# A retention layer and a two-matrix MLP in one kernel: attention steps of four blocks in place of three

## The chip, the cores and the metric

The kernel runs on one core of a Trainium2 chip. The core has five engines with instruction streams of their own: TensorE (PE, matmuls into the 8 banks of PSUM, with the weight loads, PEld, booked apart), VectorE (DVE), ScalarE (ACT), GpSimd (POOL) and SyncE (SP). POOL issues the loads that turn float32 into bfloat16 on the way, SP issues the output stores and the transposing DMAs. The metric is the device time of one execution in microseconds, lower is better.

## The reference

There are 8 batch entries, 8 heads, 576 tokens an entry and 64 channels a head. Each entry goes through retention, a causal attention without softmax that decays with the distance, and its 512 channels a token then go through an MLP with 2048 hidden channels.

```python
q, k, v: (8, 8, 576, 64);  x @ w_in: (4608, 512) @ (512, 2048);  w_out: (2048, 512)
gamma = 1.0 - 2.0 ** (-5.0 - np.arange(H))
Dmat = np.where(rel >= 0, gamma[:, None, None] ** rel[None, :, :], 0.0)
ret = scores * Dmat                       # scores = q @ k.T / 8
x = (ret @ v).transpose(0, 2, 1, 3).reshape(B * S, H * D)
h = x @ w_in
out = (h * (1.0 / (1.0 + np.exp(-1.702 * h)))) @ w_out
```

The decay factors into a part of the key's position and one of the query's: values are scaled by gamma to the power of minus their position (`scale_v`), outputs by gamma to the power of theirs (`gq`). So a block of 64 queries needs the scores inside its own block, masked to the lower triangle, and a running state, the sum of k times v over all earlier blocks of its entry.

## The kernel before

**The MLP.** The 4608 tokens are cut into 9 MLP chunks of 512. For each, 16 units of `hidden` (4 matmuls of 128x512, ACT applies the activation and writes `gT`) and 16 units of `project` (4 matmuls each; 4 units make 128 output rows, which ACT copies to `osb` and SP stores). Three buffers `osb` rotate. Each unit takes a PSUM bank; the banks named U, H0 and H1 rotate in `next_bank`. The second MLP chunk is done in two halves of 256 tokens (`hidden_half`, `units_half`), and between them two of its four output rows.

**The attention.** Entry 0 is done at the start in chunks of 128 rows. Entries 1 to 7 are done in steps that are put between MLP units, in an order written out by hand. An entry has 9 blocks of 64 tokens; a step is 3 blocks, so there are 21 steps (`NWIDE`). Its matmuls are 64x64x64 and use one of four quarters of PE each: row half by where the operands lie, column half by where the result goes. To use all four within one block, `load_shifted` (L222) puts the k and v of heads 4 to 7 64 rows lower than those of heads 0 to 3, as two DMAs a tensor and chunk; an entry takes 5 chunks of 128 rows.

**A burst** (L587) is what PE does for a step: values and inter (the product of queries and state `zw`) for the step that is finished (`m_out`), scores and states for the next one (`m_in`). A merged burst has both, and in some places at the start they stand apart: `(burst, None, m, ...)` does only the second half, `(step, m, False)` only the first. [...] Scores go to bank pair S, outputs to O and Z, states to W and to corners of the others. After it DVE multiplies the output into `xT` (`evac_wide`, L682), masks the scores (`mask_wide`), sums the states into `zacc` (`state_wide`) and casts them to `zw`.

**Order and queues.** `run` (L956) issues units and, after unit i, what `between[i]` lists. A unit that stands ahead of a `step` also waits for everything that the step needs (`needs`), so that a burst doesn't stop in its middle. Scores need q and k with channels on the partitions: `turn` does this for the first chunks on PE, `turn_dma` (L528) for the others by transposing DMAs on SP. After step m, `turn_step(m + 3)` puts the transposes of step m + 3 into SP's queue, where each waits for its load and holds up what stands behind it; and new loads go into POOL's queue. A load waits until the sixth load ahead of it has landed (`pace`, L206). Three entries of staging (`NST`) and 10 turned chunks (`NQK`) rotate.

```python
AHEAD = 6
def pace():
    return issued[-AHEAD] if len(issued) > 3 * NC + AHEAD else None
```

Of the kernel before, what the change touches and what calls it, by code (L numbers as in the profile page):

```python
# [11 lines left out]
B = 8  # L12
# [10 lines left out]
NWIDE = 3 * (B - 1)  # L23
NSTEP = B * NC
# [107 lines left out]
def bass_retnet_parallel__then__act_gelu_quick_kernel(  # L132
# [11 lines left out]
    with es:  # L144
# [10 lines left out]
        posj = sb("posj", [P, NC], FP32)  # L155
# [6 lines left out]
        vraw = sb("vraw", [P, H, NC], FP32)  # L162
        vfac = [sb(f"vfac{i}", [P, H, NC], FP32) for i in range(2)]
        zacc = sb("zacc", [P, 3, 2 * 128], FP32)
        zw = sb("zw", [P, NBLK, 2, 2, DH], BF16)
# [8 lines left out]
        smw = [t[:, 0 : 2 * 6 * 64].rearrange("p (a x n) -> p a x n", a=2, x=6) for t in sm_all]  # L174
# [7 lines left out]
        psA = ps("psA", [P, 5, 512])  # L182
# [5 lines left out]
        psB = ps("psB", [P, 3, 512])  # L188
        psH = [psB[:, i, :] for i in range(2)]
        psU = psB[:, 2, :]  # L190
        pairs = [(psS, ["S"]),
                 (psB[:, 0:2, :].rearrange("p a (h n) -> p a h n", h=HP), [("H", 0), ("H", 1)])]

        def wide(m):
            return 1 + m // 3, m % 3
# [13 lines left out]
        def load(b, c, what="qkv"):  # L209
            sl, rows = b % NST, ROWS[c]  # L210
            for nm, src, dst in (("q", q, st_q), ("k", k, st_k), ("v", v, st_v)):
                if nm not in what:
                    continue
                if b > 0 and nm != "q":
                    load_shifted(b, c, nm, src, dst)
                    continue
                s = src[b, :, 128 * c : 128 * c + rows, :].rearrange("h p d -> p h d")
                d = dst[0:rows, sl, c, :].rearrange("p (h d) -> p h d", d=DH)
                paced(R.op("POOL", lambda e, d=d, s=s: e.dma_start(d, s),  # L219
                           w=[(nm, sl, c)], dma=(nm, sl, c), own=pace()))  # L220

        def load_shifted(b, c, nm, src, dst):  # L222


            sl = b % NST
            parts = []
            for u, (lo, hi) in enumerate(((0, ROWS[c]), (64 if c == 0 else 0, 128))):
                d = dst[lo:hi, sl, c, 256 * u : 256 * u + 256].rearrange("p (h d) -> p h d", d=DH)
                t0 = 128 * c - 64 * u
                s = src[b, 4 * u : 4 * u + 4, t0 + lo : t0 + hi, :].rearrange("h p d -> p h d")  # L230
                parts.append((d, s))
            paced(R.op("POOL", lambda e: [e.dma_start(d, s) for d, s in parts],  # L232
                       w=[(nm, sl, c)], dma=(nm, sl, c), parts=2, own=pace()))

        def load_entry(b, first=0):
            for c in range(first, NC):
                load(b, c)
# [14 lines left out]
        def iota(t, name, pattern, base, mul):  # L252
            R.op("POOL", lambda e: e.iota(t.ap(), pattern, base=base, channel_multiplier=mul,
                                          allow_small_or_imprecise_dtypes=True), w=[name])
# [22 lines left out]
        def constants_first():  # L277
            iota(posj, "posj", [[128, NC]], 0, 1)
            iota(posa, "posa", [[1, 128]], 0, 0)
            R.op("DVE", lambda e: e.tensor_tensor(  # L280
                vraw.ap(), posj.ap().unsqueeze(1).to_broadcast([P, H, NC]),
                lnh.ap().unsqueeze(2).to_broadcast([P, H, NC]), ALU.mult),
# [13 lines left out]
            for hp in range(HP):  # L296
# [6 lines left out]
                vfac[0].ap(), vraw.ap(), float(QK_SCALE), ALU.mult), r=["vraw"], w=[("vfac", 0)])  # L303
# [9 lines left out]
        def constants_shifted():  # L313
            for r in range(2):
# [4 lines left out]
            R.op("DVE", lambda e: e.tensor_copy(vfac[1][:, 0:4, :], vfac[0][:, 0:4, :]),  # L319
                 r=[("vfac", 0)], w=[("vfac", 1)])  # L320
            for h in range(4, H):
                R.op("DVE", lambda e, h=h: e.tensor_single_scalar(
                    vfac[1][:, h, :], vfac[0][:, h, :], float(gamma(h) ** 64), ALU.mult),
                    r=[("vfac", 0)], w=[("vfac", 1)])
            for t, nm in ((st_k, "k"), (st_v, "v")):
                R.op("DVE", lambda e, t=t: e.memset(t[0:64, 1:NST, 0, 256:512], 0.0),
                     w=[(nm, sl, 0) for sl in range(1, NST)])

        def constants_third(a, b):
            for t, nm in ((st_q, "q"), (st_k, "k"), (st_v, "v")):  # L330
                R.op("DVE", lambda e, t=t: e.memset(t[64:128, a:b, 4, :], 0.0),
                     w=[(nm, sl, 4) for sl in range(a, b)])
# [37 lines left out]
        def constants_mask3():  # L370
            m = mask.ap().unsqueeze(1).unsqueeze(1).to_broadcast([P, 2, 2, 128])
            f = vfac[0].ap().rearrange("p (u t j) c -> p j t u c", u=2, t=2)
            for j in range(2):
# [3 lines left out]
                     r=["mask", ("vfac", 0)], w=mask3_keys)  # L377

        def scale_v(n, eng="DVE", to=None):
            b, c = divmod(n, NC)  # L380
            sl = b % NST
            t = st_v[:, sl, c, :].rearrange("p (h d) -> p h d", d=DH)
            f = vfac[min(b, 1)][:, :, c : c + 1].to_broadcast([P, H, DH])
            if n == 0:
                i = early(1).rearrange("p (h d) -> p h d", d=DH)
                R.op(eng, lambda e: e.tensor_tensor(t, i, f, ALU.mult),
                     r=[("vfac", 0)] + early_keys(1), w=[("v", sl, c)])
                return
            if to is None:
                R.op(eng, lambda e: e.tensor_tensor(t, t, f, ALU.mult),  # L390
                     r=[("vfac", min(b, 1))], w=[("v", sl, c)])
# [3 lines left out]
                 r=[("vfac", min(b, 1)), ("v", sl, c)], w=[v3_key])  # L395

        def sides(n):
            b, c = divmod(n, NC)
            return [(0, st_q, "q", b % NST, c), (1, st_k, "k", b % NST, c)]
# [123 lines left out]
        def turn(n, own=False):  # L523
            at = next_bank() if own else None
            transposes(n, at)
            evac_t(n, at)
# [559 lines left out]
```

## Time and profile before

| | us |
|---|---|
| median of 3 runs | 299.05 (298.82 to 299.48) |
| the profiled execution, its own time | 298.93 |
| its span, first to last instruction | 297.1 |
| PE busy | 291.1 (98%) |
| DVE busy | 123.1 (41%) |
| ACT busy | 125.9 (42%) |
| POOL busy, issuing DMAs for the most part | 151.6 (51%) |
| of PE: `project` 128x512 (544 matmuls) | 122.0 |
| of PE: `hidden` 128x512 (492 matmuls) | 108.9 |
| chain of waits, share of PE | 94% |

The page gives busy time by engine, the span in 40 slices of 7.4 us (each digit the busy share in tenths), and the chain of waits, which is followed back from the last instruction to whatever released each one. In the chain and in timelines a line has the start in us, the duration, the engine, the tile and the line of the kernel (L627 states, L599 values, L615 inter, L641 scores, L732 and L749 hidden, L765 project, L533 transposing DMAs). "DMA to landing" is the time from the issue of a DMA until its last piece has arrived.

### The profile page before, as it was taken

The numbers are of one execution on the slowest core, as the hardware profiler recorded it, in microseconds if no ns is written. First come the engines' busy times: TensorE is split into PE (matmuls) and PEld (weight loads), VectorE is DVE, ScalarE is ACT, GpSimd is POOL, SyncE is SP. The second block draws the span as 40 slices with busy tenths as digits, with TensorE's granted clock in tenths as the row PEclk, the third lists the DMA queues.
The fourth block names the chain that finished last, engine by engine and source line by source line (L and its number), as shares of the span: only waits on it lengthen the run. The fifth ranks groups of instructions, "written<-read, shape, count | busy, mean of one in ns | idle before, by whom it ended". The sixth has DMA issues, their size and how long they took to land.

```text
span 297.1 us, 7697 instructions
## 1 busy us (share of the span) xinstructions
PE 291.1 (98%) x3399; PEld 148.5 (50%) x3399; DVE 123.1 (41%) x221; ACT 125.9 (42%) x208; POOL 151.6 (51%) x205
## 2 busy tenths in 40 slices
PE   7799999999999999999999999999999999999996
PEld 3464455848544444544454445545454445444444
DVE  7769475454445435532615324245326504000012
ACT  6658426617256313540355045503660275026600
POOL 8975979989959887568984797000000000000000
PEclk9999999999999999999999999999999999999999
DMA  9999999999999999999999999904820200030012
GB/s 133 156 186 190 173 171 165 188 131 140 182 140 143 183 143 175 194 130 134 154 218 124 114 188 162 85 2 108 170 38 2 107 37 2 0 108 35 0 50 93
DMA packets 154850, 36.04 MB, mean 121 GB/s; under 512 B 145472, under 2 KB 150336, under 8 KB 154816
## 3 DMA queue, kind: packets, MB, share of 16 engines
q0 software_dynamic: 116304, 18.10, 94.1%
q1 hardware_dynamic: 38512, 17.44, 32.6%
q8 instruction: 27, 0.44, 0.6%
q14 instruction: 7, 0.06, 0.1%
HBM read 36.70 MB, written 9.44 MB: 155 GB/s over the span
## 4 chain that ended last, share of the span: by engine, by line
PE 94%; POOL 2%; DMA 2%; issue 0%; DVE 0%; POOLq 0%
PE psB L765 40%; PE psB L732 36%; PE psB L749 5%; PE psA L627 2%; DMA st_k<-in_k_dram 2%; PE psA L599 2%; PE psA L641 2%; PE psA L615 1%; PE psA L765 1%; PE psA L791 1%; PE psB L843 1%; PE psA L411 1%; POOL st_k L219 1%; POOL st_q L219 1%; POOL st_v L219 1%
## 5 line engine op out<-in xcount | busy, mean ns | idle before, releaser
L765 PE MATMUL psB<-w_out_sb,gT 128*128 128x512 bf16 x544 | 122.0, 380 | 0.0
L732 PE MATMUL psB<-xT,w_in_sb 128*128 128x512 bf16 x492 | 108.9, 379 | 0.0
L737 ACT ACTIVATE gT<-psB 128x512 bf16<-128x512 f32 x123 | 73.5, 597 | 38.4 <-PE psB L732 38.1
L765 PEld LDWEIGHTS psB<-w_out_sb,gT 128*128 128x128 bf16 x544 | 51.8, 98 | 60.2 <-DVE sm L696 0.3
L732 PEld LDWEIGHTS psB<-xT,w_in_sb 128*128 128x128 bf16 x492 | 47.5, 98 | 56.5
L685 DVE TENSOR_TENSOR xT<-psA,gq 128x768 bf16<-128x768 f32 x21 | 20.1, 958 | 115.3 <-PE psA L615 115.3
L232 POOL DMA_DIRECT2D st_k<-in_k_dram x70 | 52.5, 774 | 15.2 <-DMA st_k<-in_k_dram 10.9
L774 ACT ACTIVATE osb<-psB 128x512 f32<-128x512 f32 x31 | 18.5, 597 | 90.2 <-PE psB L765 86.8
L232 POOL DMA_DIRECT2D st_v<-in_v_dram x70 | 51.9, 767 | 5.7 <-DMA st_v<-in_v_dram 3.3
L219 POOL DMA_DIRECT2D st_q<-in_q_dram x39 | 34.8, 891 | 10.2 <-DMA st_q<-in_q_dram 7.6
L390 DVE TENSOR_TENSOR st_v<-st_v,vfac 128x512 bf16<-128x512 bf16 x36 | 23.3, 681 | 1.2 <-DMA st_v<-in_v_dram 1.2
L714 DVE TENSOR_TENSOR zacc<-zacc,psA 128x256 f32<-128x256 f32 x49 | 20.5, 419 | 6.9 <-PE psA L627 5.7
L696 DVE TENSOR_TENSOR sm<-psA,maskw 128x768 bf16<-128x768 f32 x21 | 19.9, 948 | 0.0
L749 PE MATMUL psB<-xT,w_in_sb 128*128 128x256 bf16 x128 | 15.0, 273 | 0.0
L777 DVE COPY osb<-psB 128x512 f32<-128x512 f32 x3 | 2.1, 692 | 29.7 <-PE psB L765 29.7
L749 PEld LDWEIGHTS psB<-xT,w_in_sb 128*128 128x128 bf16 x128 | 12.2, 98 | 1.7
L418 ACT ACTIVATE qk<-psA 128x1024 bf16<-128x1024 bf16 x8 | 8.2, 1022 | 9.8 <-PE psA L411 9.8
L599 PE MATMUL psA<-sm,st_v 64*64 64x64 bf16 x504 | 11.8, 195 | 0.3
L627 PE MATMUL psA<-st_v,st_k 64*64 64x64 bf16 x448 | 11.8, 199 | 0.0
L627 PEld LDWEIGHTS psA<-st_v,st_k 64*64 64x64 bf16 x448 | 7.5, 105 | 8.3 <-issue 7.8
L755 ACT ACTIVATE gT<-psB 128x512 bf16<-128x512 f32 x16 | 9.4, 599 | 5.0 <-PE psB L749 5.0
L615 PE MATMUL psA<-qk,zw 64*64 64x64 bf16 x448 | 11.1, 194 | 0.0
(103 smaller groups left out, 164.3 us busy)
## 6 DMA issues: line engine op xcount, KB each, us to landing
out_dram<-osb SPq DMA_DIRECT2D x35, 256.0 KB, 3.9
st_q<-in_q_dram POOLq DMA_DIRECT2D x31, 128.0 KB, 7.5
st_k<-in_k_dram POOLq DMA_DIRECT2D x57, 64.0 KB, 7.3
st_v<-in_v_dram POOLq DMA_DIRECT2D x57, 64.0 KB, 7.0
w_out_sb<-in_moe_w_out_dram POOLq DMA_DIRECT2D x4, 512.0 KB, 10.9
w_in_sb<-in_moe_w_in_dram POOLq DMA_DIRECT2D x3, 512.0 KB, 8.6
st_k<-in_k_dram POOLq DMA_DIRECT2D x4, 128.0 KB, 4.8
w_in_sb<-in_moe_w_in_dram POOLq DMA_DIRECT2D x2, 256.0 KB, 6.8
```

The source lines that it names most:

```text
L219: paced(R.op("POOL", lambda e, d=d, s=s: e.dma_start(d, s), w=[(nm, sl, c)], dma=(nm, sl, c), own=pace()))
L232: paced(R.op("POOL", lambda e: [e.dma_start(d, s) for d, s in parts], w=[(nm, sl, c)], dma=(nm, sl, c), parts=2, own=pace()))
L390: R.op(eng, lambda e: e.tensor_tensor(t, t, f, ALU.mult), r=[("vfac", min(b, 1))], w=[("v", sl, c)])
L627: i = e.matmul(psA[half(j), bank, off + 64 * t : off + 64 * t + 64], rows_of(st_k, m_in, g, u, h), rows_of(st_v, m_in, g, u, h), start=(t ...
L685: R.op("DVE", lambda e: e.tensor_tensor(xT[:, :, t0 : t0 + 192].rearrange("p (u j) n -> p u j n", u=2), psA[:, 2:4, 0:384].rearrange("p u ...
L696: R.op("DVE", lambda e: e.tensor_tensor(o, i, k, ALU.mult), r=["maskw"], w=[("sm", si(m))], ps=["S"])
L714: R.op("DVE", lambda e, to=to, src=src, was=was: e.tensor_tensor(to, was, src, ALU.add), r=[("zacc", (blk - 1) % 3)], w=[("zacc", blk)], p ...
L732: i = e.matmul(bank, w_in_sb[:, a, 128 * f : 128 * f + 128], xT[:, a, 512 * c : 512 * c + 512], start=(a == 0), stop=(a == 3))
L737: R.op("ACT", lambda e: e.activation(gT[c % 2][:, f, :], bank, AF.Gelu_apprx_sigmoid), w=[("gT", c % 2, f)], ps=[key])
L749: m = e.matmul(bank[:, 256 * i : 256 * i + 256], w_in_sb[:, a, 128 * (f + i) : 128 * (f + i) + 128], xT[:, a, a0 : a0 + 256], start=(a == ...
L765: i = e.matmul(bank, gT[c % 2][:, f, 128 * r : 128 * r + 128], w_out_sb[:, f, :], start=(f == 0), stop=(f == NF - 1))
L774: R.op("ACT", lambda e: e.activation(osb[m].ap(), bank, AF.Copy), w=[("osb", m)], ps=[key])
```

## The change

Entries 1 to 7 become one line of 63 blocks, loaded in 32 chunks of 128 rows without the shift; chunks 4, 13 and 22 hold the end of one entry and the start of the next. A step is four blocks, so there are 16 steps. In place of the two head groups of one block, an even and an odd block now fill the four quarters together: outputs of even blocks go to bank O, of odd blocks to Z; states of even blocks to W, of odd blocks to U (Z where the burst stands alone). U is lent by the MLP, whose units leave it alone around a merged burst (`without`), while banks are taken by the order of last use (`lru`). `project` units of one row now come one after the other on two banks. From the third MLP chunk on there are two steps a chunk, after units 10 and 24; in the second, steps are placed by hand again. Step 3 is marked urgent: its output goes ahead of the states on DVE. The mask covers 8 x 64 columns for each half instead of 6 x 64, and the second set of factors (`vfac[1]`), the zero fills of the shifted corners and the PE transpose of chunk 9 go.

```diff
-NWIDE = 3 * (B - 1)
-NSTEP = B * NC
+NLIN = (B - 1) * NBLK
+NWIDE = (NLIN + 3) // 4
+NLOAD = (NLIN + 1) // 2
...
+        smw = [t.ap().rearrange("p (a x n) -> p a x n", a=2, x=8) for t in sm_all]
...
-        psA = ps("psA", [P, 5, 512])
+        psA = ps("psA", [P, 6, 512])
...
-        psB = ps("psB", [P, 3, 512])
...
+        psU = psA[:, 5, :]
...
+        def slot(N):
+            return divmod((N + NC) % (NST * NC), NC)
+
+        def rows_in(N):
+            return min(128, 64 * (NLIN - 2 * N))
+
+        def load_next(N):
+
+            if N >= NLOAD:
+                return
+            sl, c = slot(N)
+            b, p0 = 1 + 128 * N // S, 128 * N % S
+            pieces = [(0, b, p0, min(128, S - p0))]
+            if pieces[0][3] < rows_in(N):
+                pieces.append((64, b + 1, 0, 64))
+            for nm, src, dst in (("q", q, st_q), ("k", k, st_k), ("v", v, st_v)):
+                parts = []
+                for lo, e0, t0, n in pieces:
+                    s = src[e0, :, t0 : t0 + n, :].rearrange("h p d -> p h d")
+                    parts.append((dst[lo : lo + n, sl, c, :].rearrange("p (h d) -> p h d", d=DH), s))
+                paced(R.op("POOL", lambda e, parts=parts: [e.dma_start(d, s) for d, s in parts],
+                           w=[(nm, sl, c)], dma=(nm, sl, c), parts=len(parts), own=pace()))
...
+        def turn_dma(N):
+            n = NC + N
+            rows = rows_in(N)
+            for a, t, nm, sl, c in sides(n)[::-1]:
+                R.op("SP", lambda e, a=a, t=t, sl=sl, c=c: e.dma_start_transpose(
                     out=qk[n % NQK][:, a, :, 0:rows], in_=t[0:rows, sl, c, :]),
                     r=[(nm, sl, c)], w=[("qk", n % NQK, a)], dma=("turn", n % NQK, a))
 
...
         def blocks(m):
-            return range(3 * (m % 3), 3 * (m % 3) + 3)
...
+            return [(G % 4, G, G % NBLK) for G in range(4 * m, min(4 * m + 4, NLIN))]
...
+            return sorted({G // 2 for _, G, _ in blocks(m)})
+
...
+        def zbanks(fresh):
+            return ((4, "W"), (3, "Z") if fresh else (5, "U"))
 
...
+                r += stored(m_in, "kv") + turned_keys(m_in, 0) + turned_keys(m_in, 1)
...
+            def pairs_of(m):
+                bs = blocks(m)
+                return [bs[i : i + 2] for i in range(0, len(bs), 2)]
+
+            def state(e):
+                first = opening()
+                for two in pairs_of(m_in):
+                    for u in range(2):
                         for t in range(2):
+                            for blk, G, g in two:
+                                if g == NBLK - 1:
+                                    continue
+                                at = 256 * (blk // 2) + 128 * u + 64 * t
+                                bank = zb[blk % 2][0]
+                                for j in range(2):
+                                    h = 4 * u + 2 * t + j
+                                    i = e.matmul(psA[half(j), bank, at : at + 64],
+                                                 rows_of(st_k, G, h), rows_of(st_v, G, h),
+                                                 start=first(bank, j), stop=False,
+                                                 skip_group_check=True)
                 return i
 
...
+            def inter(e, same):
+                i = None
+                for two in pairs_of(m_out):
+                    for u in range(2):
+                        for blk, G, g in two:
+                            if g == 0:
+                                continue
+                            j = G % 2 if same else 1 - G % 2
+                            for t in range(2):
+                                i = e.matmul(out_at(G, u, j, t), zw[half(j), (G - 1) % 8, u, t, :],
+                                             turned_of(G, j, 0, u, t),
+                                             start=False, stop=not same, skip_group_check=True)
+                return i
...
+                R.op("PE", state, r=stored(m_in, "kv"), ps=[key for _, key in zb])
...
                 done = R.op("PE", phase_x, r=ro, ps=["O", "Z"])
...
+                R.op("PE", score, r=turned_keys(m_in, 0) + turned_keys(m_in, 1), ps=["S"])
...
+                R.op("PE", lambda e: inter(e, False), r=ro, ps=["O", "Z"], own=done)
+                if urgent or m_in is None:
+                    evac_wide(m_out)
+            if m_in is not None:
+                state_wide(m_in, zb, cast == "ACT")
+                if m_out is not None and not urgent:
+                    evac_wide(m_out)
                 mask_wide(m_in)
+                if cast != "ACT":
+                    cast_wide(m_in)
...
+        def state_wide(m, zb, on_act):
+            for blk, G, g in blocks(m):
+                if g == NBLK - 1:
+                    continue
+                bank, key = zb[blk % 2]
+                src = psA[:, bank, 256 * (blk // 2) : 256 * (blk // 2) + 256]
+                to, was = zacc[:, blk, :], zacc[:, (blk - 1) % 4, :]
...
+        load_next(0)
         load_w_out(2)
-        load(1, 1)
+        load_next(1)
         load_w_out(3)
-        load_entry(1, 2)
-        load_entry(2)
+        for N in range(2, 10):
+            load_next(N)
...
 
-        turns = [1]
-
-        def next_bank():
-            turns[0] += 1
-            return wide_banks[(1, 2, 0)[turns[0] % 3]]
+        lru = [0, 1, 2]
+
+        def next_bank(without=()):
+            x = next(x for x in lru if x not in without)
+            lru.remove(x)
+            lru.append(x)
+            return wide_banks[x]
 
...
-            if m > 1:
+            for N in range(10, 15):
+                load_next(N)
+
+        def step(m, into=True, cast="DVE", urgent=False):
+            burst(m, m + 1 if into and m + 1 < NWIDE else None, cast, urgent)
+            if m > 0:
                 turn_step(m + 3)
-            for c in ((0,), (1, 2), (3, 4))[i]:
-                if b + NST < B:
-                    load(b + NST, c)
+            load_next(2 * m + 15)
+            load_next(2 * m + 16)
 
         def turn_step(m):
             if m < NWIDE:
-                b, i = 1 + m // 3, m % 3
-                for n, which in (((0, "k"), (0, "q"), (1, "k"), (1, "q")),
-                                 ((2, "k"), (2, "q"), (3, "k")),
-                                 ((3, "q"), (4, "k"), (4, "q")))[i]:
-                    turn_dma(NC * b + n, which)
+                for N in chunks(m):
+                    turn_dma(N)
 
...
         def run(units, between):
+            joined = [i for i in between for fn, *args in between[i]
+                      if fn is step and (len(args) < 2 or args[1])]
             for i, unit in enumerate(units):
                 ahead = []
                 for fn, *args in between.get(i, ()):
                     if fn is step:
                         ahead += needs(args[0], args[0] + 1 if (len(args) < 2 or args[1])
                                        and args[0] + 1 < NWIDE else None)
-                unit(ahead)
+                unit(ahead, (0,) if any(k <= i <= k + 3 for k in joined) else ())
                 while later:
                     later.pop(0)()
                 for fn, *args in between.get(i, ()):
                     fn(*args)
 
...
-        def units_o(c, rows, eng="ACT"):
+        def units_o(c, rows):
             banks = {}
 
             def unit(r, g):
-                def go(ahead):
+                def go(ahead, without):
                     if g == 0:
-                        banks[r] = next_bank()
-                    project(c, r, g, *banks[r], eng=eng, ahead=ahead)
+                        banks[r] = next_bank((0,))
+                    project(c, r, g, *banks[r], eng="ACT", ahead=ahead)
                 return go
-            first = rows[:3]
-            return ([unit(r, g) for g in range(4) for r in first]
-                    + [unit(r, g) for r in rows[3:] for g in range(4)])
+            return [unit(r, g) for r in rows for g in range(4)]
 
         first = {r: next_bank() for r in (1, 2, 3)}
         first[0] = wide_banks[3]
-        run([lambda ahead, r=r, g=g: project(0, r, g, *first[r], eng="ACT", ahead=ahead)
+        run([lambda ahead, without, r=r, g=g: project(0, r, g, *first[r], eng="ACT", ahead=ahead)
              for g in range(4) for r in range(4)],
             {1: [(tail_turn,)], 3: [(intra, 4)], 5: [(turn, 5), (tail_out,), (regroup, 2)],
              7: [(scale_v, 5), (turn, 6)], 8: [(scale_v, 6), (regroup, 3)], 9: [(burst, None, 0, "ACT")],
              12: [(turn, 7)], 13: [(step, 0, False)], 14: [(scale_v, 7)], 15: [(turn, 8)]})
+        turn_step(2)
         turn_step(3)
-        turn_step(4)
         run(units_half(1, 0),
-            {0: [(turn, 9, True), (scale_v, 8), (scale_v, 9)], 1: [(burst, None, 1, "ACT")],
-             5: [(step, 1)]})
-        run(units_o(1, (0, 1)), {3: [(scale, 3)], 5: [(step, 2, False)]})
-        run(units_half(1, 1), {2: [(burst, None, 3, "ACT")], 4: [(scale, 4)]})
-        run(units_o(1, (2, 3)), {0: [(step, 3, True, "ACT")], 5: [(step, 4, False)], 6: [(scale, 5)]})
...
+            {0: [(scale_v, 8)], 1: [(burst, None, 1, "ACT")], 5: [(step, 1, False)]})
+        run(units_o(1, (0, 1)), {3: [(scale, 2)], 6: [(burst, None, 2, "ACT")]})
+        run(units_half(1, 1), {1: [(scale, 3)], 5: [(step, 2)]})
+        run(units_o(1, (2, 3)), {2: [(scale, 4)], 5: [(step, 3, True, "DVE", True)]})
+
+        for c in range(2, NCH):
             at = {}
-            for i, m in enumerate(steps):
-                u = (5, 15, 25)[i] if len(steps) == 3 else (8, 22)[i]
-                at[u - 4] = [(scale, m + 1)]
-                at[u] = [(step, m)]
-            region(c, at)
-        run(units_h(NCH - 1), {})
-        for r in range(3):
-            bank = next_bank()
-            for g in range(4):
-                project(NCH - 1, r, g, *bank)
+            for u, m in ((10, 2 * c), (24, 2 * c + 1)):
+                if c < NCH - 1:
+                    at[u - 5] = [(scale, m + 1)]
+                    at[u] = [(step, m)]
+            rows = range(4) if c < NCH - 1 else range(3)
+            run(units_h(c) + units_o(c, rows), at)
         project_pieces(NCH - 1, 3, [(psA[:, 2, :], "O"), (psW, "W")])
```

## The prediction

> **What bounds the kernel now.** I read the page first: busy shares, then the 40 slices. PE is busy in all but the first and last slices and has its full granted clock; so has the DMA row up to about 200 us, and POOL up to about 165 us.
>
> ```profile
> PE   7799999999999999999999999999999999999996
> ...
> POOL 8975979989959887568984797000000000000000
> PEclk9999999999999999999999999999999999999999
> DMA  9999999999999999999999999904820200030012
> ```
>
> To see: PE sets the end, but for the first two thirds the DMA engines are as full as PE, so an earlier demand for data can't simply be met earlier. The chain of waits names nearly only PE; here is its stretch around one merged burst (88 small matmuls), between two MLP pieces:
>
> ```profile
> 75.42 0.86 PE psB L765 x4
> 76.29 0.19 PE psA L627 x8
> 76.47 0.13 PE psA L599 x16
> ...
> 77.11 0.07 PE psA L615 x6
> 77.18 4.42 PE psB L765 x20
> ```
>
> To see: 0.89 us from 76.29 to 77.18, no wait on either side. Asked for PE's waits from 55 to 90 us, the profile has none: every transposed chunk is in time today. How closely, SP's transposes and their times to landing tell (issue, duration on SP; then the issues of the stretches 69.1 to 69.3 us and 78.0 to 78.2 us):
>
> ```profile
> 67.95 1.19 SPq L533 DMA_TRANSPOSE qk<-st_k  x1
> 69.19 1.64 SPq L533 DMA_TRANSPOSE qk<-st_q  x1
> ...
> 78.11 1.31 SPq L533 DMA_TRANSPOSE qk<-st_q  x1
> ```
>
> ```profile
> qk<-st_q SPq DMA_TRANSPOSE x1, 6.7
> ```
>
> ```profile
> qk<-st_q SPq DMA_TRANSPOSE x1, 7.1
> ```
>
> To see: a transpose lands some 7 us after its issue (the page's median over all is 7.6). Chunk 3 of entry 2 is turned (k 6.6 us after 67.95, so at 74.6; q at 75.8) when PE opens the unit that needs its k at 75.42. That is 0.8 us of slack.
>
> **The change part by part.** The profiled execution is 297.1 us of span in 298.93 us (1.83 around it), 0.12 under the median of 299.05. Sums below go against 298.93.
>
> *Small matmuls.* Their number stays (504 values, 504 scores, 448 states, 448 inters). In the chain a merged burst of 88 takes 0.89 us and one of 96 (92.60 to 93.56) 0.96, so 8.2 ns a matmul; a gap of 0.09 us ahead of each is booked on the MLP piece. A burst of 128 is 0.89 + 40 x 0.0082 + 0.09 = 1.31 us. Blocks left out of a pair (no state after an entry's last block, no inter before its first) leave two of four tiles idle and save nothing. Before: 17 merged, 4 in only (0.51 to 0.58), 4 out only (0.71 to 0.78), 21.0 in the chain + 25 x 0.09 = 23.3 us. After: 13 merged (one 0.13 shorter), 3 in only at 0.66 + 0.09 (0.58 + 16 x 0.0082, less two waits of PE on itself), 3 out only at 0.90 + 0.09: 22.1. Gain 1.2, and 1.55 of gain lies after the third MLP chunk's start at 84.21 (before 16.9, after 11 x 1.31 + 1.0 - 0.1). The transpose of chunk 9 on PE goes: 8 matmuls, 0.45.
>
> *VectorE.* Four sums of 0.42 instead of three, two output multiplications of 0.69 (nearest row: L518, 512 elements) for one of 0.96, a mask of 1.22 (L441, 1024 elements) for 0.95, a cast of 0.9: some 6 us a step against PE's 13 to 15. Hidden, except at two places. (a) Step 1's mask: states end 0.5 us after the burst starts, 1.75 + 1.22 more makes 3.5; PE is there after 0.75 + 3 x 0.87 = 3.3: wait 0.25. (b) Step 3 is urgent: both outputs come ahead of the sums. From the burst's end 0.14 + 1.3 + 1.33 (block 17 is an entry's last: two sums and a copy) = 2.75. The fourth sum frees bank U, and the third MLP chunk's first unit takes just that bank (the order of use leaves it oldest), two units or 1.73 us after the burst: wait 1.0. Bounds: 0, if the first unit had another bank, and 1.5.
>
> *ScalarE.* With two MLP banks a unit's Gelu must end within the next unit: it starts 0.42 after the last matmul, takes 0.597, and PE comes back 1.08 after: fits, by some 0.02 us, and only one unit a chunk is so placed. Output copies of 0.597 per 3.46 us are covered. If the cover fails, 0.05 each, 0.4 in all. The last chunk's copies on ScalarE instead of VectorE are off the path.
>
> *Loads.* POOL issues one DMA for a tensor of a chunk instead of two halves: 70 + 70 + 39 instructions shrink by 70, at 0.77 each. Whether that brings data sooner depends on who is the limit. POOL never paused from 46 to 58 us; but the DMA engines had the work queued: time to landing rose from 3 us (issues of 44 to 47 us) to 7 (62 to 66) and 10 (76 to 80).
>
> ```profile
> 46.00:58.00 12.00, 11.92 (x263) 8.96 (x261) 5.05 (x9) 9.12 (x15) 12.00 (x17) 1.00 1.83 186
> 58.00:70.00 12.00, 11.92 (x133) 7.32 (x120) 5.35 (x8) 3.45 (x6) 10.76 (x16) 1.00 2.31 131
> ```
>
> (Busy time of PE, PEld, DVE, ACT, POOL; clock; DMA share, over 1 where transfers overlap; GB/s.) From the landing of the last load of chunk 3 (47.8) to the turned q at 75.8 I count 16.5 loads of 128 rows, 8 transposes and 4 output stores: 28.5 pieces in 28.0 us, 0.98 each. [...] POOL's wait of 3.3 us for a memset (L326) near 22 us goes too; next in line there is the DMA queue, which holds weights till 42 us, so nothing is counted.
>
> On SP the transposes of chunks 8 and 9 now stand ahead of the second MLP chunk's first two output stores, which go out at about 76 instead of 74.5; ScalarE wants their buffers back at 88 at the earliest and they land some 7 us after issue, so this is covered by 4 us.
>
> *Demand.* This decides. Steps of four blocks on the same places of the second MLP chunk want 12 blocks at 66.5, 16 at 72.5, 20 at about 81; before it was 12 at 70.4, 15 at 75.4, 18 at 86.7. A unit ahead of a step waits for all its keys, both chunks' q and k turned. Chunks numbered along the line from 0, the last load of chunk 3 lands at 48.3 (64 more rows). Turned q of chunk 5 has 18 pieces ahead (6 loads, 4 in flight past them by the pace of six, 4 transposes, 4 stores): 66. Of chunk 7: 28 pieces, 75.7; of chunk 9: 38, 85.5. The other bound is by latency: k of chunk 7 lands after 17 pieces at 65.0, q is issued 1.3 later, lands after 7.4: 73.7; chunk 9 (27 pieces): 83.5. I take the middle, 74.7 and 84.5, since both rows are equally near.
>
> The walk: the second MLP chunk starts at 51.1 (before 50.85, plus 0.08 and 0.20 on step 0's two bursts). First half 8 x 0.87 + 0.75 + 1.0 + 0.25 = 8.95: 60.1. Seven projection units: 66.1, burst 0.75 and a wait of 0.2 on chunk 5's turn, one unit: 67.9. Five half units: 72.3; wait for chunk 7 till 74.7, **2.4**. Unit, burst 1.31, two units, five units: 82.9; wait for chunk 9 till 84.5, **1.6**. Unit, burst, two units 3.9, bank U 1.0: 89.4, where before had 84.2. That is 5.2 later, less 1.55 gained afterwards: +3.65. Time 298.93 + 3.65 = 302.6; with the bounds of the turns 301.6 to 303.6. From there on loads are ahead (chunk 11 turned at about 96, wanted at 98).
>
> **The rivals.**
>
> *Data in time* (other side: faster). If the transposes of chunk 7 land by 72.3 and of chunk 9 by 80.1, only (a) and (b) stay: 84.2 + 1.0 at the third chunk, +1.0 - 1.55, so about 298.3. It decides from a piece time of 0.85 us down. For it: POOL's 12.00 of 12.00, and fewer, larger DMAs; against it: the DMA row at 9 and the rising time to landing. Chance 0.17.
>
> *One wait instead of two*: transposes overtake queued loads (issues at 76 to 80 us: loads 10, transposes 7.1 to 8.3), chunk 7 by 73.5, chunk 9 by 82: 299.5 to 300.9. Chance 0.14.
>
> *The clock drops in the wait.* With PE idle for 2.4 us or more the clock could be withdrawn and take some us to return. No run here shows it: the longest waits of before, up to 1.6 us near the start, left the granted clock at 1.00. If some 3 us of matmuls ran at half rate the time would be 304.1 to 305.6. [...] Chance 0.10.
>
> *Tiles lose their overlap.* Two matmuls in a row now share a row half (before, a column half). If only two of four tiles ran at once, 8.2 ns would be 16 and the 1900 matmuls cost 15 us more: 314. Against it: all four tiles stay in each group of four. Chance 0.04.
>
> **How the numbers follow.** Forecast 302.6 (0.55, within 301 to 304), rivals as above. What a measurement can tell from no change is about 0.2%, 0.6 us. Faster is nearly all of the first rival, 0.16; same takes its edge and a little of the second, 0.05; slower the rest, 0.79. The range goes from 298.2 (takes in most of the first) to 305.2 (part of the third); the forecast's own is 301 to 304.
>
> **What would show it.** Right: PE waits on transposes of qk near 72 and 82 us and a wait at the third chunk's first unit on the sum in zacc; chain pieces of bursts of 1.2 us; 16 steps; POOL far less busy, but times to landing of 7 us or more up to 85 us. Wrong: PE without waits from 60 to 90 us (data in time), a PEclk digit under 9, bursts of 2 us, or new waits in the later chunks.

## The result: 4.2% slower, and the profile after

The changed kernel takes 311.88 us (median of four runs, 310.99 to 313.20) where the kernel before took 299.26 beside it: a ratio of 1.042, 95% interval 1.038 to 1.047. The forecast was 302.6, range 298.2 to 305.2: the direction was right, the size was not. The profiled run took 312.06 us, span 310.3, so 13.1 us more than the profiled run of before. Here and below an execution that lies over 1.5% above the fastest of its kernel (one of run 5's four) is left out of times and ratios.

From the page of the changed kernel (the rows of 40 slices of 7.8 us, then the queue that carries instructions: transfers, MB, share of 16 engines):

```profile
PE   8899998996947999999999999999999999999996
...
POOL 8999059633654556835863200000000000000000
PEclk9999999999796999999999999999999999999999
DMA  9999999999999999999999936206610110010002
...
q8 instruction: 27, 0.44, 0.6%
```

Nearly all the loss lies in slices 10 to 13, from 70 to 100 us: PE is partly idle there and its granted clock falls, which in the kernel before never happened ahead of the end. POOL has become slack (109.8 us busy, before 151.6); the DMA engines are as full as they were (the DMA row shows nothing but 9 up to 178 us, before up to 193). The waits of PE from 40 to 110 us (in total, how often, the longest; the kernel before has none in that window):

```profile
PE psA L633 <- issue: 6.6, 2, 5.9
PE psB L755 <- DMA qk<-st_q: 2.8, 1, 2.8
PE psA L614 <- issue: 0.8, 1, 0.8
PE psB L771 <- DMA qk<-st_q: 0.5, 1, 0.5
PE psB L771 <- DVE sm L701: 0.2, 1, 0.2
```

Lines 2 to 5 are waits that the prediction named: chunk 7's transpose, chunk 5's (a semaphore wait, though the row names no releaser), chunk 9's, step 1's mask. The first, and largest, is not in it. The chain of waits shows where it lies:

```profile
78.86 8.11 DMA qk<-st_q
86.97 0.35 issue
87.33 1.02 PE psB L771 x4
...
89.12 0.27 PE psA L614 x31
89.38 0.10 PE psA L633 x8
89.48 5.88 issue
95.37 0.32 PE psA L633 x7
95.69 3.30 PE psB L771 x8
98.98 0.86 PE psA L738 x4
...
108.48 0.37 PE psA L600 x32
```

PE stops for 5.88 us between two matmuls of one loop (`inter`, L633), where no semaphore stands. Behind it eight matmuls of 512 columns take 3.30 us instead of 1.73. The third MLP chunk starts at 98.98 us, before at 84.21. From there to the end the changed kernel needs 211.3 us and the one before needed 212.9.

The granted clock around the first of the two long pauses, in stretches (busy time of PE, PEld, DVE, ACT, POOL, then the clock, DMA share and GB/s):

```profile
74.20:76.60 2.40, 0.00 (x0) 0.00 (x0) 0.00 (x0) 0.60 (x1) 1.60 (x2) 1.00 2.09 155
...
77.50:78.50 1.00, 1.00 (x52) 0.77 (x54) 0.00 (x0) 0.42 (x1) 1.00 (x2) 0.82 3.30 139
78.50:79.50 1.00, 1.00 (x92) 1.00 (x80) 0.86 (x3) 0.17 (x1) 1.00 (x2) 0.50 2.81 147
...
81.50:82.50 1.00, 1.00 (x10) 0.80 (x8) 1.00 (x2) 0.60 (x1) 0.49 (x1) 0.97 3.34 101
```

PE's last matmul ahead of the wait ended at 74.20 us and its next began at 77.01. After this idle time of 2.81 us (the 2.8 in the list of waits) PE ran at half clock from 78.15 to 81.56 us, although it had been at work again for 1.1 us. Around the second pause the clock was 0.50 from 91.80 to 98.63 us.

### The profile page after: what moved, and what is told of

Read it like the earlier page. It is cut to its first block, busy times and chain, and to the rows that moved or that the text cites. A ratio compares the mean times of both kernels' runs of the same rounds, so it can differ in the third digit from the quotient of the medians.

```text
span 310.3 us, 7594 instructions
## 1 busy us (share of the span) xinstructions
PE 293.6 (95%) x3391; PEld 149.0 (48%) x3391; DVE 118.5 (38%) x221; ACT 126.1 (41%) x208; POOL 109.8 (35%) x136
## 4 chain that ended last, share of the span: by engine, by line
PE 70%; DMA 17%; POOL 9%; issue 3%; DVE 1%; SPq 0%; POOLq 0%
PE psB L771 32%; PE psB L738 21%; PE psA L738 10%; DMA st_k<-in_k_dram 9%; DMA st_q<-in_q_dram 5%; DMA qk<-st_q 3%; POOL st_q L237 2%; POOL st_v L237 2%; POOL st_k L237 2%; PE psA L633 1%; PE psA L600 1%; PE psA L646 1%; PE psA L797 1%; POOL st_k L214 1%; POOL st_q L214 1%
## 5 line engine op out<-in xcount | busy, mean ns | idle before, releaser
L738 PE MATMUL psB<-xT,w_in_sb 128*128 128x512 bf16 x332 | 79.1, 380 | 0.0
L743 ACT ACTIVATE gT<-psB 128x512 bf16<-128x512 f32 x83 | 49.6, 597 | 29.8 <-PE psB L738 29.6
L738 PEld LDWEIGHTS psB<-xT,w_in_sb 128*128 128x128 bf16 x332 | 31.5, 98 | 38.6 <-ACT gT L743 1.9
L738 PE MATMUL psA<-xT,w_in_sb 128*128 128x512 bf16 x164 | 41.9, 380 | 0.0
L237 POOL DMA_DIRECT2D st_v<-in_v_dram x35 | 30.8, 882 | 17.6 <-DMA st_v<-in_v_dram 13.8
L237 POOL DMA_DIRECT2D st_k<-in_k_dram x35 | 29.8, 853 | 17.3 <-DMA st_k<-in_k_dram 14.8
L743 ACT ACTIVATE gT<-psA 128x512 bf16<-128x512 f32 x41 | 24.4, 599 | 10.1 <-PE psA L738 10.1
L738 PEld LDWEIGHTS psA<-xT,w_in_sb 128*128 128x128 bf16 x164 | 15.9, 98 | 19.1 <-issue 0.3
L701 DVE TENSOR_TENSOR sm<-psA,maskw 128x1024 bf16<-128x1024 f32 (+2 forms) x17 | 19.6, 1152 | 0.0
L682 DVE TENSOR_TENSOR xT<-psA,gq 128x512 bf16<-128x512 f32 x20 | 12.8, 684 | 16.2 <-PE psA L633 16.2
L633 PE MATMUL psA<-qk,zw 64*64 64x64 bf16 x448 | 11.3, 201 | 6.9 <-issue 6.6
## 6 DMA issues: line engine op xcount, KB each, us to landing
w_out_sb<-in_moe_w_out_dram POOLq DMA_DIRECT2D x4, 512.0 KB, 14.8
```

The source lines that it names most:

```text
L237: paced(R.op("POOL", lambda e, parts=parts: [e.dma_start(d, s) for d, s in parts], w=[(nm, sl, c)], dma=(nm, sl, c), parts=len(parts), own ...
L633: i = e.matmul(out_at(G, u, j, t), zw[half(j), (G - 1) % 8, u, t, :], turned_of(G, j, 0, u, t), start=False, stop=not same, skip_group_che ...
L682: R.op("DVE", lambda e, o=o, i=i, k=k: e.tensor_tensor(o, i, k, ALU.mult), r=[("gq", 0), ("gq", 1)], w=[("xT", t0 // 64 + blk) for blk, _, ...
L701: R.op("DVE", lambda e, o=o, i=i, k=k: e.tensor_tensor(o, i, k, ALU.mult), r=["maskw"], w=[("sm", si(m))], ps=["S"])
L738: i = e.matmul(bank, w_in_sb[:, a, 128 * f : 128 * f + 128], xT[:, a, 512 * c : 512 * c + 512], start=(a == 0), stop=(a == 3))
L743: R.op("ACT", lambda e: e.activation(gT[c % 2][:, f, :], bank, AF.Gelu_apprx_sigmoid), w=[("gT", c % 2, f)], ps=[key])
```

## The experiments

Two theories stood at the start. **Theory 1, late instructions.** The page counts 27 transfers of 16384 bytes on the instruction queue. PE has 6855 recorded instructions (a matmul and its weight load are two), which is 26.8 times 256. In the changed kernel each piece up to 185 us starts only after PE has passed a border of 256 instructions, the one before the border that needs the piece; below, this passing counts as the asking. (Later, and in runs 5 and 12 from 65 us on, some pieces start up to 3.8 us ahead of it.) A burst of 128 runs through its 256 instructions in 1.22 us (from 169.19 us on), and if the piece is late PE stops. **Theory 2**: the stop belongs to the burst itself or to late data, and the instructions' place in the program doesn't matter.

**1. 124 idle instructions near the start.** `fill(n)` is the idle matmul of 512 columns; `tick` is new:

```
-        fill(11)
+        fill(9)
+        tick(64)      # 64 matmuls of 64 x 64, 64 columns, on the idle tile
```

> The changed kernel with 124 more instructions on PE near its start, where PE still waits for its first data: two of the eleven idle matmuls of 512 columns are replaced by 64 idle matmuls of 64 columns (each with its weight load). Nothing else differs. Late instructions (theory 1): PE's instructions are brought in by DMAs of 16384 bytes, 256 instructions each, and the 5.88 us in the middle of a burst at 89.48 us is a piece that came late, because the piece before had been entered only 5.0 us earlier. With 124 instructions more, the border that now lies at the 2242nd PE instruction falls 124 instructions earlier, into the middle of the burst, and the border before it into the burst before, some 9 us earlier: no stop at 89 us. In exchange two borders come 3.7 us apart near 104 us: a stop of 0 to 4 us there. Time 311.9 - 7.5 + 2 = 306.4, between 304 and 309. Late transposes or something in the burst itself (theory 2): the instructions before the burst can't matter, the stop stays at the same matmul, 311.9.

Measured 309.05 us, ratio 1.033 (1.029 to 1.037): 2.8 less than the changed kernel, at the very edge (309) of what theory 1 gave. The stop at 89 us is gone. PE's waits from 40 to 160 us:

```profile
PE psA L633 <- issue: 3.4, 1, 3.4
PE psA L738 <- issue: 1.4, 1, 1.4
PE psB L771 <- DMA qk<-st_q: 1.0, 1, 1.0
PE psA L738 <- DVE zacc L717: 0.7, 1, 0.7
PE psA L614 <- issue: 0.7, 1, 0.7
```

The stops have moved to other lines: 3.4 us at the 1474th PE instruction (57.5 us, not expected), 1.4 at the 2754th (106.2 us, expected near 104), 0.3 at the 3522nd, 0.7 at the 3778th. The changed kernel's stops were at the 962nd and the 2242nd. All six numbers leave 194 when divided by 256. Since the 3.4 us came ahead of it, the wait for chunk 7 (2.8 us in the changed kernel) vanished: here the stop covered the later wait for data.

**2. 240 idle instructions**, the same with `fill(7)` and `tick(124)`.

> The same with 240 more instructions (four idle matmuls of 512 columns replaced by 124 of 64). Late instructions (theory 1): now one border lies just ahead of the burst at 88 us and the next just behind it, 2.3 us apart by the trace of the changed kernel: the stop leaves the middle of the burst and lies in the MLP units behind it, and is longer, 7 to 9 us. Other borders less than 4 us apart come only at 222 us, when the DMA engines are half empty. Time 311.9 + 2 = 314, between 312 and 316. Theory 2: 311.9 with the stop at the same matmul as before.

Measured 313.12 us, ratio 1.046 (1.042 to 1.051), within the range of theory 1. Its chain of waits around the burst:

```profile
90.62 0.16 PE psA L633 x15
90.78 0.32 PE psB L771
91.10 3.38 issue
94.48 1.87 PE psB L771 x4
```

The burst runs through; the stop has moved into the MLP unit behind it, at instruction 2498, which again leaves 194. It is 3.4 us, not 7 to 9; the wait for chunk 7 was longer here, 4.2 us. Idle instructions 70 us earlier move the stop by counts of 256, so theory 2 falls.

**3. Step 3 in two.**

```
-   run(units_o(1, (2, 3)), {2: [(scale, 4)], 5: [(step, 3, True, "DVE", True)]})
+   run(units_o(1, (2, 3)), {2: [(scale, 4)], 5: [(step, 3, False)]})
...
+            if c == 2:
+                at[2] = [(burst, None, 4, "ACT")]
```

> The changed kernel, but the burst that gives out step 3 and takes in step 4 in the second MLP chunk is made in two: step 3 is only given out there, and step 4 is taken in by a burst of its own at the third unit of the third MLP chunk. Chunks 8 and 9 of the line are then wanted some 6 us later, and no burst of 128 comes until 108 us. Both theories: no wait for chunk 9 (0.7 us), no stop of 5.88 us and no MLP units at half clock behind it (1.6 us); the second burst costs 0.35 us. Time 311.9 - 0.7 - 5.9 - 1.6 + 0.35 = 304.1. The wait for chunk 7 near 74 us and the low clock behind it stay.

Measured 304.78 us, ratio 1.018 (1.013 to 1.022), 0.7 over what was expected. No stop, no wait for chunk 9; the wait for chunk 7 (4.2 us idle) and half clock behind it (0.50 from 78 to 83 us) remain.

**4. Steps 2 and 3 in two.** In addition:

```
-   run(units_half(1, 1), {1: [(scale, 3)], 5: [(step, 2)]})
-   run(units_o(1, (2, 3)), {2: [(scale, 4)], ...
+   run(units_half(1, 1), {1: [(scale, 3)], 5: [(step, 2, False)]})
+   run(units_o(1, (2, 3)), {1: [(burst, None, 3, "ACT")], 2: [(scale, 4)], ...
```

> As the run before, and step 2 in the same way: given out at its place, and step 3 taken in by a burst of its own, four units later. Chunk 7 is then wanted 3.5 us later. Late transposes explain the wait of 2.4 us near 74 us: it goes, and with it the granted clock of 0.5 between 78 and 81.5 us, worth some 2 us; the second burst costs 0.35. Time 304.1 - 2.5 - 2 + 0.35 = 300.0. If the clock of 0.5 has another cause than the wait, it stays and the time is 302.

Measured 302.37 us, ratio 1.008 (1.005 to 1.012), 2.4 over the expectation. The wait for chunk 7 is gone and the clock row shows nothing but 9, so the low clock went with the wait. What is left of PE's waits:

```profile
PE psA L614 <- issue: 1.0, 1, 1.0
PE psB L771 <- issue: 0.9, 1, 0.9
PE psA L633 <- issue: 0.6, 1, 0.6
```

The first is a semaphore of the burst that takes in step 2 (chunk 5's transpose; the changed kernel has the same 0.8). The other two are stops at instructions 1986 and 962, again at borders.

**5. Three loads in flight.** `AHEAD = 6` becomes `AHEAD = 3`.

> The changed kernel with one number changed: POOL keeps three loads in flight instead of six (AHEAD). If the late instruction pieces and the late transposes stand behind queued loads (six of 0.98 us each), both get shorter: time to landing of a load from 8.3 to about 5 us, of a transpose from 8.1 to about 5, the time from one instruction border to the next piece from 10.9 us to about 6, so no or under 1 us of stop at 89 us (5.88), no wait for chunk 7 (2.4 to 3.9), no low clock (2 + 1.6): time 311.9 - 11 = 301, between 299 and 304. If three in flight don't keep the DMA engines busy, chunks come later than 0.98 us a load and the wait for chunk 7 grows instead: over 312.

Measured 310.55 us, ratio 1.034 (1.026 to 1.042): nearly as slow as the changed kernel, for another reason. A line of the page's DMA issues (KB, median us to landing; before the edit 8.3) and PE's waits from 40 to 110 us:

```profile
st_k<-in_k_dram POOLq DMA_DIRECT2D x32, 128.0 KB, 4.9
```

```profile
PE psB L755 <- DMA qk<-st_q: 3.7, 1, 3.7
PE psA L614 <- DMA qk<-st_q: 2.2, 1, 2.2
```

Loads land sooner after issue, and no stop at a border is left: the pieces asked for at 84.0 and 90.3 us were written 1.5 and 1.2 us later, where the changed kernel's at 78.1 and 84.5 took 4.3 and 8.8. But chunks come later. Between 40 and 80 us 24.6 times 128 KB came in on POOL's queue, in the changed kernel 29.4: 16% less. Fewer loads in flight bought earlier instructions with later data.

**6. PE kept busy through the wait.** On the kernel of run 3:

```
-   run(units_half(1, 1), {1: [(scale, 3)], 5: [(step, 2)]})
+   run(units_half(1, 1), {1: [(scale, 3)], 4: [(fill, 14, (psA[:, 2, :], "O"))], 5: [(step, 2)]})
```

> The kernel with step 3 made in two (304.8), and 14 idle matmuls of 512 columns (14 x 0.216 = 3.0 us) on PE right ahead of the unit that waits for chunk 7 (3.84 us in that run, 2.4 in the changed kernel's profile). They don't change when the data comes. If the granted clock of 0.5 to 0.8 between 78 and 81.5 us comes from PE's idling, it is 1.00 here, and the units behind the wait take their usual time: 304.8 - 2 = 302.8. If it has another cause (the dense bursts, DMA), the clock falls all the same: 304.8, or a little over.

Measured 308.90 us, ratio 1.029 (1.024 to 1.035): 4 us slower than run 3, not 2 faster. For the clock it does decide (stretches of PE's busy time, clock, DMA share, GB/s):

```profile
74.00:76.70 2.70, 2.67 (x13) 1.00 2.23 137
76.70:77.40 0.70, 0.00 (x0) 1.00 2.42 154
...
78.40:79.40 1.00, 1.00 (x88) 1.00 2.66 140
```

With only 1.0 us idle (76.67 to 77.71 us) the clock stays at 1.00 through the burst, where in run 3 it was 0.50. The loss is theory 1 once more: the 14 idle matmuls are 28 instructions, and they brought two borders to either side of the burst. PE stopped for 3.4 us at instruction 1986, and behind that stop the clock fell after all (0.50 at 85 to 87 us).

**7. One unit later, and 240 idle instructions**, on the kernel of run 4: `6: [(burst, None, 2, "ACT")]` becomes `7: ...`, and `fill(7)`, `tick(124)`.

> The kernel with steps 2 and 3 made in two (302.4), with two waits more taken away: step 2 is taken in one unit later (in that run it waited 1.0 us for chunk 5's transpose), and 240 instructions more at the start move the instruction borders: their nearest distance is then 5.9 us (at 49 us) and 6.5 to 7 us, where it was 5.6 and 5.8. By the theory of late instructions the stops of 0.59 and 0.88 us shrink by about half. 302.4 - 1.0 - 0.7 = 300.7. If it is slower than before still, what is left is small waits, not the bursts' own cost.

Measured 303.78 us, ratio 1.014 (1.008 to 1.019): slower than run 4. Chunk 5's wait and one stop are gone, 0.5 us of stops is left, and a new wait of 2.7 us of PE on ScalarE stands at 87.2 us. ScalarE, in its own rows:

```profile
89.21 0.60 ACT L780 ACTIVATE osb<-psB 128x512 f32<-128x512 f32 x1 [7.15 <-DMA out_dram<-osb]
```

It waits for an output store. SP issued that store only at 81.4 us, since the transposes of chunks 8 and 9 stand ahead of it and wait for their loads.

**8. The kernel before, with 166 idle instructions** (`fill(8)`, `tick(86)`).

> The kernel before, with 166 more instructions on PE near its start: three of the eleven idle matmuls of 512 columns replaced by 86 of 64. Late instructions (theory 1): its trace shows instruction borders at least 6.7 us apart from 40 us on, and no stop. Moved by 166 instructions, two borders come 4.6 us apart at 57.8 us and two 5.7 us apart at 82 us. With the 6 to 11 us from a border to the next piece that the stops of the other runs showed, it stops for 1 to 4 us at the first and 0 to 3 us at the second: 299.5 + 3 = 302.5, between 300.5 and 306. If only the changed kernel's bursts of 128 can starve PE, nothing changes: 299.5.

Measured 299.73 us, ratio 0.999 (0.997 to 1.002): nothing. A miss. The borders did come 4.61 us apart at 58 us and 5.93 apart at 82.5 us, but the pieces were written 2.8 and 4.3 us after being asked for, and PE never stopped. So here a short distance alone didn't stop PE; at the changed kernel's stop of 5.88 us the piece was slow too, 8.8 us. From 40 to 125 us a piece took 4.0 us on average (6.2 at most) in the kernel before, 4.4 (6.0) here, and 5.5 (8.8) in the changed kernel; in the changed kernel's stops PE went on 2.1 and 1.6 us after the piece was written. Why the pieces of the changed kernel took longer, with six loads in flight as before, is open.

**9. The stores ahead.** On run 7, the transposes of chunks 8 and 9 move on SP behind the second MLP chunk's first two stores:

```
-            if m > 0:
+            if m > 1:
                 turn_step(m + 3)
...
+                                7: [(burst, None, 2, "ACT"), (turn_step, 4)]
```

> The run with steps 2 and 3 made in two, step 2 taken in a unit later and 240 idle instructions (303.8), with the transposes of chunks 8 and 9 moved on SP behind the second MLP chunk's first two output stores. In that run the stores were issued at 81.4 and 82.0 us behind the transposes, ScalarE waited 7.15 us for the buffer of the first, PE 2.65 us for ScalarE, and the granted clock was 0.5 from 91.4 to 94.4 us. With the stores ahead of the transposes both go: 303.8 - 2.65 - 1.5 = 299.6, as the kernel before. If the transposes then come late for the burst of step 4 at about 90 us, up to 2 us come back there.

**10. The same with `AHEAD = 5`.**

> The run with the transposes of chunks 8 and 9 behind the stores, and five loads in flight instead of six. The backlog that instruction pieces and transposes stand behind is shorter by 0.98 us; with three in flight loads came 19% slower. If five still fill the DMA engines: 0.3 to 0.5 us less of stops at instruction borders, 299.2; if they don't, chunks come later, and the time is 300 to 302.

Measured 305.30 us, ratio 1.019 (1.016 to 1.023), and 303.04, ratio 1.010 (1.007 to 1.014): both over what was expected. ScalarE's wait is gone in both. In run 9 the unit ahead of step 4 waits 1.7 us for a transpose near 97 us (the expectation's up to 2), in run 10 0.6. But in both PE's granted clock shows a 7 between 15 and 30 us, and the second MLP chunk begins at 53.1 and 54.3 us instead of 52.0. Each fall comes with an idle time of PE there: 1.81 us in run 9 (from 13.85 us, a load of k was late), 2.57 in run 10 (from 20.99 us, `w_in` was late), and 1.72 in run 5, which shows the same fall without idle instructions. Why these loads came late is open; run 8 has idle instructions and no idle time over 1.1 us there. In run 9 PE also stops for 0.4 us at a border (90.0 us). The five loads in flight can't be judged from this pair. (The 19% in the second expectation is wrong; it is the 16% of run 5.)

**11. Loads held back.** In the changed kernel the loads of chunk 11 and later wait for PE's last instruction of step 3's burst:

```
+            if N >= 11 and hold is not None:
+                hold.append(N)
+                return
...
+        def release():          # called at the end of step 3
+            free.append(R.q["PE"][-1])
+            late, hold = hold, None
+            for N in late:
+                load_next(N)
```

In this kernel the transposes of chunks 11 to 13 (issued from 86.6 to 95.6 us) stand ahead of the held loads (issued from 92.0 us on) and turn what lay in the buffers, so these chunks' turned q and k are not their own: the run tells times and is no usable kernel. Between 81 and 89 us SP issued four transposes, as many as in the changed kernel.

> The changed kernel with the loads of chunk 11 and later held back until PE has finished the burst that gives out step 3 (the one with the stop of 5.88 us); before that POOL has nothing to issue after chunk 10. PE's instruction stream is the same, so the borders lie where they lay. If the piece for the border inside that burst is late because it stands behind loads in flight, it now comes some 3 us after the border before instead of 8.8, and the stop shrinks from 5.88 to under 1 us, with the low clock behind it gone (1.6); chunk 9's transposes are quicker too (0.7). 311.9 - 5 - 1.6 - 0.7 = 304.6, between 303 and 306; the wait of 2.4 to 3.9 us for chunk 7 and its low clock stay. If the loads have nothing to do with it (the distance of the borders alone decides), the stop stays at 4 us or more: 311. A new wait for chunk 11 near 100 us would add up to 3 us to either.

Measured 306.59 us, ratio 1.020 (1.016 to 1.025), 0.6 over the range, with a longer wait for chunk 7 (4.9 us). Its chain of waits at the burst that had the stop:

```profile
90.64 0.13 PE psA L639 x16
90.77 0.28 PE psA L620 x31
91.05 0.20 PE psA L639 x15
91.25 0.02 issue
91.27 1.29 DVE xT L688 x2
...
93.25 0.43 DVE zacc L723
93.69 0.05 issue
93.73 1.04 PE psA L744 x4
```

The instruction stream is the same and the borders were even closer, 4.3 us instead of 5.0. The piece was written 2.4 us after it was asked for instead of 8.8, and the stop of 5.88 us is gone. Runs 8 and 11 together: the stop of 5.88 us took both, borders 5.0 us apart and a piece that came 8.8 us after it was asked for, with the loads in flight, and 2.4 us with them held back.

**12. What helped, together**, with no idle instructions: runs 4, 9's order on SP, step 2 taken in a unit later, `AHEAD = 5`, and step 4 at the third MLP chunk's unit 13 instead of 10.

> All that helped, together: steps 2 and 3 made in two, step 2 taken in a unit later, the transposes of chunks 8 and 9 behind the stores, five loads in flight, step 4 three units later in the third MLP chunk (the two runs before waited 0.6 and 1.7 us there), and no idle instructions at the start (in those runs the second MLP chunk began 1 to 2 us later than in the other runs, with a low granted clock near 20 us). 303.0 - 2 - 0.7 = 300.3, within 299 and 302: level with the kernel before, since two split bursts cost 0.7 and the bursts' own gain is 1.2 to 1.6.

Measured 300.06 us against 300.35 beside it, ratio 0.9997 (0.998 to 1.001): level with the kernel before, as expected. PE shows no wait over 0.2 us from 40 us on, and its clock row only 9. No run beat the kernel before.

## Why the prediction was right in direction and wrong in size

**Where the 13.1 us are.** The walk of the prediction put the third MLP chunk 5.2 us later; it was 14.8. Measured against predicted, in us: stops at instruction borders 6.6 (0.70 and 5.88) against nothing; half clock 3.2 (1.7 near 80 us, 1.5 near 97 us, each the time at low clock times what was withheld) against nothing; chunk 7's wait 2.8 against 2.4; chunk 9's 0.5 against 1.6; chunk 5's 0.8 against 0.2; step 1's mask 0.2 against 0.25; bank U 0 against 1.0. The excess is 8.6 of the 9.6; 1.0 stays unbooked.

**The step that failed** is *Small matmuls*: "A burst of 128 is 0.89 + 40 x 0.0082 + 0.09 = 1.31 us". As the price of a burst it holds (1.29 us from 108.48 us on, no gap). But it priced the 256 instructions of a burst at PE's rate alone and never asked where they come from. Merging spaces the bursts out and packs each more densely, so that a border was reached 5.0 us after the last, while the next piece took 8.8 (in the kernel before, from 40 to 125 us, 6.7 at least and 6.2 at most). Each stop ended 1.2 to 2.1 us after the piece asked for one border earlier was written. That loads in flight make the piece late is shown by runs 5 and 11: with fewer of them, pieces were written 1.5, 1.2 and 2.4 us after being asked for, in the changed kernel 4.3 and 8.8.

**The rival of the clock** was priced about rightly (by the author's estimate 1.5 to 3 us, measured 1.7 and 1.5) and given too little, 0.10. It came true twice, once behind the data wait that the forecast itself held. An idle time of 2.81 us was enough here and one of 1.72 us in run 5; 1.44 us in run 1 was not, nor were the waits of before that the prediction went by (PE's own longest was 1.32 us; the 1.6 is of its weight loads). Run 6 shows the cause: with PE kept busy but for 1.0 us the clock stayed at 1.00, where it was 0.50 in run 3.

**Demand** was right: chunk 7 cost 2.8 us of idle PE (predicted 2.4, by its bounds 1.4 to 3.4), and 4.2 to 4.9 in runs 2, 3 and 11; chunk 9 late by less, since PE came to it late itself. Its causes were right too: runs 3 and 4 take these waits away by asking later, and POOL's slack, for whose 70 issues the prediction counted no gain, bought nothing: a load of q landed 8.3 us after its issue (the page's median for 128 KB; before 7.5). **Bank U** took 0.7 us in runs 1, 5 and 11 (predicted 1.0). In the changed kernel no such wait shows; the eight matmuls at half clock ahead of it probably gave VectorE the time. **The gain** after the third MLP chunk's start is 1.6 us, predicted 1.55: the change does what its counts say, and the first 100 us take it back many times over. **The output stores** on SP, costed at nothing with a cover of 4 us, were issued at 80.2 us instead of 76; the cover just held, and run 7 shows the price once it doesn't, 2.7 us and the clock.

## What to carry to other kernels

Price an instruction stream in instructions, not only in engine time: here a stretch ran through 256 of them in 5.0 us while the next transfer of 16384 bytes, with loads in flight, took 8.8, and the engine stopped in mid-loop for 5.9 us, the difference and 2.1 us more. A stop booked as "issue" with no semaphore, at an instruction count that leaves the same rest modulo 256 (194 here, in all thirteen), was that in these runs. When work is merged and asked for earlier while transfers are the limit, cost the waits with what follows them: the clock (3.2 us here), and whatever sits behind the late transfer on its issuing queue (2.7 us in run 7).

## What was not expected of the hardware

From 20 us on, thirteen stops of PE of 0.25 us and more, in eight kernels and at five lines of the program, have no releaser in the trace and no semaphore that they waited for. All lie at PE records that leave 194 modulo 256 (in run 9, where matmul records are missing, by the count of weight loads). In each, PE went on 1.2 to 2.1 us after the piece was written, so the length of a stop is a sum: 8.8 us to the piece and 2.1 behind it, less 5.0 from border to border, are the 5.9 us of the changed kernel.

The length of a single idle time doesn't decide about the clock in these runs: 1.72 us (run 5) was followed by half clock, 1.83 us in run 3 (at 20.9 us) wasn't. The fall can come after PE is at work again: in the changed kernel it came 1.1 us after, at 78.15 us. There the clock stayed at 0.50 for 3.41 us after the first idle time (2.81 us) and for 6.83 us, from 91.80 us on, in and after the second (5.88 us). What decides whether an idle time of some 2 us costs anything is not shown.
